# Linear attention and a squared-ReLU MLP on one core: moving two features, two sets of transposes and one batch of loads in a hand-written order

## The chip, the core and the metric

The kernel runs on one core of a Trainium2 chip. Its time is the device time of one execution in microseconds (us); given is the median of several runs. One execution was also profiled: its record gives the span, from the first to the last instruction, and its own time, which is a little longer.

The engines of the core run beside one another, each in its own order: TensorE (PE, with PEld for its weight loads), VectorE (DVE), ScalarE (ACT), GpSimd (POOL) and SyncE (SP). An engine waits on semaphores for what it needs, and everything behind a waiting instruction on that engine waits too. SP here only issues DMAs; POOL issues others.

## The reference

```python
r = np.maximum(x, 0.0)                                  # phi(x), x = q or k
phi = np.concatenate([r * cos, r * sin], axis=-1)       # cos, sin by position
kv  = np.einsum('bhsf,bhsd->bhfd', k_p, v)
z   = np.sum(k_p, axis=2)
num = np.einsum('bhsf,bhfd->bhsd', q_p, kv)
den = np.einsum('bhsf,bhf->bhs', q_p, z)[..., None] + 1e-06
x   = (num / den)            # then (batch*seq, heads*dim) = (4608, 512)
h   = x @ w_in               # 512 -> 2048
g   = relu(h) ** 2
out = g @ w_out              # 2048 -> 512, float32
```

q, k and v are float32 of (8 batches, 8 heads, 576 positions, 64 dims).

## The kernel before

The 576 positions of a batch are cut into four pieces of 128 positions (`j` = 0 to 3, all 8 heads) and a tail of 64 positions (`j` = 4, two groups of 4 heads on the two halves of the partitions). For each batch the work is:

- `load_batch`: one DMA of 1 MB and two of 64 KB for each of q, k and v. The input tiles have two buffers each.
- `att_k`: for a piece of k, a cosine half (relu, then times a column; on VectorE by `feat_cos`, L171, or on ScalarE by `feat_cos_act`, L186) and a sine half (`feat_sin`, ScalarE, L181). `att_v` copies v into bf16 beside a column of ones (L198 or L200).
- `att_kv`: 40 small matmuls into `kz` (L241), part 0 for j = 0 and 1, part 1 for the rest, then a copy to `kvz` on ScalarE (L249). The ones give the sum z.
- `att_feat` and `att_qT`: the same features for q, and a transposing DMA on SP (L267), one for j = 0 and 1, one for 2 and 3, one for the tail.
- `att_d`: `att_num`, 8 matmuls (L310), then `att_div` on VectorE (L320 to L324), which gives x. `att_x`: x is transposed by a DMA on SP (L342).
- `gemm1`: x times w_in in steps of 8 or 10 per batch. Each step's matmuls (L383) fill a PSUM tile `hps`, ScalarE takes its relu (`rt`, L391), VectorE squares it (`gT`, L398). `hps` has two buffers, so step n + 2 needs rt of step n.
- `gemm2`: g times w_out. From batch 1's second pair of row tiles on it is done by `pair_mm`, in which seven products of half-size blocks take the place of eight; it needs sums of blocks (`g_sum`, L521, and `w2_sum`, L506, on VectorE), copies of partial products on ScalarE (`s`, L561 and L576) and additions on VectorE (`u`, `ysb`, L537). Two of its four PSUM tiles (`yu`, `yv`) are in the two buffers of `hps`.

The order of the work is written out by hand. The main loop runs over **slots**: one slot is one step of gemm1 or gemm2. Slots 0 to 7 are gemm1 of batch 0, 8 to 15 its gemm2; 16 to 25 gemm1 of batch 1 and 26 to 33 its gemm2; 34 to 41 gemm1 of batch 2, 42 to 49 its gemm2; 50 to 59 gemm1 of batch 3. The attention of a later batch is hung behind these slots with `at(slot, function, ...)`. Within a slot the pieces run in the order of the `at` calls; the square of a gemm1 step follows its slot's pieces. `plan(b, k, f, kv, d, ...)` takes the slots of one batch: k for the key and value pieces, f for the query features and their transposes, kv for the two parts of kz, d for num, division and x transposes.

Each engine gets its instructions in this order. So SP, too, issues its DMAs strictly in order: query transposes, x transposes and, from batch 4 on, the loads. The loads of batches 1 to 3 go through POOL.

PSUM has one more buffer of note: `kz` and `num` share one (`pa`), so each needs the reader of the one before to be done.

Of the kernel before, what the change touches and what calls it, by code (L numbers as in the profile page):

```python
# [19 lines left out]
def kernel(  # L20
# [9 lines left out]
    nc = tc.nc  # L30
# [13 lines left out]
    NS = J + 1  # L44
# [562 lines left out]
    slots, first, second = [], {}, {}  # L607
# [6 lines left out]
    def at(s, fn, *args):  # L614
        after.setdefault(s, []).append((fn, args))
# [6 lines left out]
        att_qT_pe(b, j)  # L622
        att_qT_copy(b, j)

    def plan(b, k, f, kv, d, t=(), x=(), shared=True):


        for j in range(NS):
            last = j == J or j % 2
            at(k[j], att_k, b, j, feat_cos_act if shared and j % 2 else feat_cos)  # L630
            at(k[j], att_v, b, j, nc.scalar if shared and (b > 2 or j % 2) else nc.vector)
            at(f[j], att_feat, b, j)
            if t:
                at(t[j], att_t, b, j)
            elif last:
                at(f[j], att_qT, b, j // 2)
            at(d[j], att_d, b, j)
            if x:
                at(x[j], att_x_pe, b, j, x[j] > 16)
            elif last:  # L640
                at(d[j], att_x, b, j // 2)
        for i in range(2):
            at(kv[i], att_kv, b, i)


    for j in (2, 3):
# [8 lines left out]
    at(18, att_d, 0, J)  # L655
    at(19, att_x_pe, 0, J, True)
    plan(
        1,
        k=(8, 8, 8, 9, 9),
        f=(4, 5, 6, 12, 13),  # L660
        kv=(10, 10),
        d=(11, 13, 15, 17, 19),
        t=(5, 6, 7, 16, 17),
        x=(12, 14, 16, 18, 20),
        shared=False,
    )
    at(14, load_batch, 3, nc.gpsimd, "qkv")
    plan(
        2,
        k=(21, 22, 23, 24, 25),  # L670
        f=(18, 19, 20, 22, 23),
        kv=(26, 26),
        d=(27, 28, 29, 31, 33),
    )
    plan(
        3,
        k=(30, 32, 33, 34, 35),
        f=(27, 29, 31, 32, 33),
        kv=(36, 36),
        d=(37, 38, 39, 40, 41),  # L680
    )
    for b in range(4, B):
        o, p = second[b - 2], first[b - 1]
        at(second[b - 3] + 6, load_batch, b, nc.sync, "kv")
        at(first[b - 2] + 9, load_batch, b, nc.sync, "q")
        plan(
            b,
            k=(o, o, o + 1, o + 1, o + 2),
            f=(o + 4, o + 4, o + 5, o + 5, o + 6),
            kv=(o + 3, o + 4),  # L690
            d=[p + j for j in range(NS)],
        )
# [96 lines left out]
```

## Time and profile before

| what | value |
|---|---|
| median of 5 runs | 293.88 us (293.3 to 295.98) |
| the profiled execution's own time | 294.83 us |
| its span | 293.0 us |
| granted clock of TensorE | 1.0 throughout |
| TensorE busy | 281.2 us |
| VectorE busy | 201.6 us |
| ScalarE busy | 164.7 us |
| GpSimd busy | 39.2 us |

Busy shares are averages over the whole span. The waits of an engine say after whom it stood idle and for how long. In the timeline a row gives start, length, engine, line, operation and tile, and behind it in brackets the idle time just before and what ended it. An instruction's length there is longer than the distance to the next one on the same engine, since neighbours overlap: ScalarE's sine or cosine of a full piece takes 0.71 us and the next one starts after 0.61. DMA rows of SP show how long issuing took; the landing is told apart from it.

### The profile page before, as it was taken

How to read it: one execution, taken by the hardware profiler on the slowest of the kernel's cores; microseconds unless marked ns; L12 is line 12 of the kernel's file. 1: busy time of each engine (PE TensorE's matmuls, PEld its weight loads, DVE VectorE, ACT ScalarE, POOL GpSimd, SP SyncE). 2: the span in 40 equal slices, each digit the busy share in tenths (PEclk: the TensorE clock that was granted, in tenths of full speed). 3: DMA queues.
4: the chain of work that ended last, by engine and by line, in shares of the span. 5: the costliest groups of instructions: out<-in, count | busy, mean ns of one | idle time of the engine just before them, and what ended most of it. 6: DMA issues, size and time to landing. Idle time of an engine off the chain costs nothing.

```text
span 293.0 us, 7285 instructions
## 1 busy us (share of the span) xinstructions
PE 281.2 (96%) x3038; PEld 236.4 (81%) x3045; DVE 201.6 (69%) x450; ACT 164.7 (56%) x251; POOL 39.2 (13%) x67
## 2 busy tenths in 40 slices
PE   8989999998999979999999999999999999999994
PEld 3569855888677968898998888988998988889883
DVE  1367765596399486977688686977677877546584
ACT  3476653679748747745693258845595551155210
POOL 1462504750000000000002000000001000000011
PEclk9999999999999999999999999999999999999999
DMA  6999995999749988799619995199808520300014
GB/s 213 284 204 284 354 214 170 342 361 266 133 116 162 289 146 155 214 284 285 183 59 194 271 258 165 74 242 322 231 6 200 146 46 2 138 7 2 0 73 144
DMA packets 76641, 53.04 MB, mean 181 GB/s; under 512 B 52000, under 2 KB 71712, under 8 KB 76608
## 3 DMA queue, kind: packets, MB, share of 16 engines
q1 hardware_dynamic: 66816, 29.24, 43.4%
q0 software_dynamic: 9648, 23.20, 26.8%
q8 instruction: 24, 0.39, 0.5%
q10 hardware_dynamic: 144, 0.13, 0.1%
q14 instruction: 9, 0.07, 0.1%
HBM read 36.70 MB, written 9.44 MB: 157 GB/s over the span
## 4 chain that ended last, share of the span: by engine, by line
PE 83%; DVE 5%; DMA 5%; ACT 3%; SPq 2%; issue 1%; DVEq 0%
PE hps L383 41%; PE ya L525 9%; PE yc L525 8%; PE yu L525 7%; PE yv L525 4%; PE num L310 3%; DMA q<-in_q_dram 3%; PE kz L241 3%; PE yps L432 2%; PE yh L432 2%; PE yps L456 2%; DMA qpT<-qpt 2%; DVE ysb L537 1%; ACT rt L391 1%; PE tq L284 1%; SPq L69 1%
## 5 line engine op out<-in xcount | busy, mean ns | idle before, releaser
L383 PEld LDWEIGHTS <-w1sb 128*128 128x128 bf16 x1312 | 112.9, 98 | 13.7 <-issue 2.9
L383 PE MATMUL hps<-xT,w1sb 128*128 128x256 bf16 (+1 forms) x1056 | 119.0, 269 | 1.1 <-DVE ysb L537 0.6
L391 ACT ACTIVATE rt<-hps 128x1024 bf16<-128x1024 f32 x72 | 73.6, 1023 | 66.8 <-PE hps L383 43.4
L398 DVE TENSOR_TENSOR gT<-rt 128x1024 bf16<-128x1024 bf16 x64 | 44.0, 687 | 21.3 <-ACT rt L391 21.2
L525 PEld LDWEIGHTS <-gs 128*128 128x128 bf16 x480 | 46.9, 98 | 5.5
L525 PEld LDWEIGHTS <-gT 128*128 128x128 bf16 x312 | 29.8, 98 | 3.5
L410 POOL DMA_DIRECT2D out_dram<-ysb x14 | 7.6, 547 | 174.4 <-DVE ysb L537 146.9
L181 ACT ACTIVATE kp<-k,sin_col 128x512 bf16<-128x512 f32 x32 | 22.4, 717 | 3.1 <-DMA k<-in_k_dram 3.1
L324 DVE TENSOR_TENSOR x<-num,rden 128x512 bf16<-128x512 f32 x32 | 22.1, 691 | 1.1
L181 ACT ACTIVATE qp<-q,sin_col 128x512 bf16<-128x512 f32 x32 | 22.1, 721 | 1.2 <-DMA q<-in_q_dram 1.2
L320 DVE TENSOR_SCALAR den<-num 128x8 f32<-128x8 f32 (+1 forms) x40 | 6.6, 164 | 22.3 <-PE num L310 22.3
L521 DVE TENSOR_TENSOR gs<-gT 128x1024 bf16<-128x1024 bf16 x26 | 17.8, 685 | 0.0
L171 DVE TENSOR_SCALAR qp<-q,cos_col 128x512 bf16<-128x512 f32 x32 | 14.7, 487 | 1.7 <-DMA q<-in_q_dram 1.7
L383 PE MATMUL hps<-xTt,w1sb 128*128 128x128 bf16 x256 | 15.1, 219 | 0.8 <-ACT rt L391 0.8
L525 PE MATMUL yc<-w2sb,gs 128*128 128x256 bf16 x120 | 15.6, 272 | 0.0
L525 PE MATMUL yu<-w2sb,gs 128*128 128x256 bf16 x120 | 15.6, 272 | 0.0
L525 PE MATMUL ya<-w2t,gs 128*128 128x256 bf16 x120 | 15.6, 273 | 0.0
L525 PE MATMUL yu<-w2t,gs 128*128 128x256 bf16 x120 | 15.5, 272 | 0.0
L200 ACT CAST vext<-v 128x512 bf16<-128x512 f32 x23 | 14.1, 614 | 1.9 <-DMA v<-in_v_dram 1.9
L576 ACT COPY s<-yu 128x256 f32<-128x256 f32 x15 | 5.6, 372 | 16.7 <-PE yu L525 16.7
L310 PEld LDWEIGHTS <-qpT 128*128 128x128 bf16 (+1 forms) x240 | 10.3, 100 | 5.1 <-DMA qpT<-qpt 2.8
L310 PE MATMUL num<-kvz,qpT 128*128 128x65 bf16 (+1 forms) x240 | 11.7, 194 | 2.6 <-DMA qpT<-qpt 2.6
(93 smaller groups left out, 338.1 us busy)
## 6 DMA issues: line engine op xcount, KB each, us to landing
out_dram<-ysb POOLq DMA_DIRECT2D x14, 512.0 KB, 3.9
k<-in_k_dram SPq DMA_DIRECT2D x5, 1024.0 KB, 7.9
v<-in_v_dram SPq DMA_DIRECT2D x5, 1024.0 KB, 8.5
q<-in_q_dram SPq DMA_DIRECT2D x5, 1024.0 KB, 5.5
q<-in_q_dram POOLq DMA_DIRECT2D x3, 1024.0 KB, 12.4
k<-in_k_dram POOLq DMA_DIRECT2D x3, 1024.0 KB, 9.9
v<-in_v_dram POOLq DMA_DIRECT2D x3, 1024.0 KB, 10.0
w1sb<-in_moe_w_in_dram POOLq DMA_DIRECT2D x4, 512.0 KB, 9.3
```

The lines of the kernel that those rows point to most:

```text
L171: nc.vector.tensor_scalar(out=dst[:, :, 0:D], in0=src, scalar1=0.0, scalar2=cos_col[:, j : j + 1], op0=ALU.max, op1=ALU.mult,)
L181: nc.scalar.activation(out=dst[:, :, D:F], in_=src, func=ACTF.Relu, scale=sin_col[:, j : j + 1])
L200: copy(out=vx[:, j, h0:h1, 0:D], in_=piece("v", b, j)[:, h0:h1, :])
L241: nc.tensor.matmul(out=kz[:, half, hh * E1 : (hh + 1) * E1], lhsT=lhsT, rhs=rhs, start=(j == 0 and hh == 0), stop=(j == J and hh == HH - 1),)
L310: nc.tensor.matmul(out=out, lhsT=lhsT, rhs=kvz[:, half * HH + hh, :], start=True, stop=True)
L324: nc.vector.tensor_tensor(out=x_of(b, j).rearrange("p (b k) (l d) -> p b k l d", b=n, l=2), in0=n4[:, :, :, 0:D].rearrange("p b (k l) d -> ...
L383: nc.tensor.matmul(out=out, lhsT=w1sb[:, kb, hb * P : (hb + 1) * P], rhs=rhs, start=(kb == 0), stop=(kb == KB - 1),)
L391: nc.scalar.activation(out=rt[:, :, :], in_=hps[:, :, :], func=ACTF.Relu)
L398: nc.vector.tensor_tensor(out=dst, in0=rt[:, :, :], in1=rt[:, :, :], op=ALU.mult)
L432: nc.tensor.matmul(out=ypss[b][tt], lhsT=gTs[b][:, hb, tt * P : (tt + 1) * P], rhs=w2sb[:, hb, :], start=(hb == 0), stop=(hb == HB - 1),)
L521: nc.vector.tensor_tensor(out=t[:, :, :], in0=in0, in1=in1, op=op)
L525: nc.tensor.matmul(out=acc, lhsT=lhs[:, hb, :], rhs=rhs[:, hb, :], start=(hb == 0), stop=(hb == HB2 - 1),)
```

## The change

Four groups of slots and engines in the plan change; no instruction is added or taken away but for the engine that does some features.

- Batch 2: the cosine halves of k for j = 1 and 3 go from ScalarE to VectorE. All else of batch 2 stays.
- Batch 3: the cosine halves of k for j = 0, 1 and 2 are on ScalarE (before: 1 and 3), the rest on VectorE. The key pieces and the query features take other slots; query pieces 2, 3 and the tail are in slots 33 and 34 (before 31 to 33), and both of their transposes in slot 34. Part 1 of kz goes from slot 36 to 37. The nums and divisions go from slots 37 to 41 to slots 38 to 41 and 43, with their x transposes.
- Batch 4: the loads of k and v go from slot 32 to 34, where they stand behind batch 3's query transposes. On SP the order was: transpose of query pieces 2 and 3, k, kt, kt, v, vt, vt, transpose of batch 2's last x, transpose of the query tail. It becomes: transpose of batch 2's last x, of query pieces 2 and 3, of the query tail, then k, kt, kt, v, vt, vt.
- Batch 4's q stays in slot 43, but on SP it now comes after the tail x transpose of batch 3, which is in the same slot.

```diff
-    def plan(b, k, f, kv, d, t=(), x=(), shared=True):
+    def plan(b, k, f, kv, d, t=(), x=(), act_cos=(1, 3), act_v=range(NS)):
         for j in range(NS):
             last = j == J or j % 2
-            at(k[j], att_k, b, j, feat_cos_act if shared and j % 2 else feat_cos)
-            at(k[j], att_v, b, j, nc.scalar if shared and (b > 2 or j % 2) else nc.vector)
+            at(k[j], att_k, b, j, feat_cos_act if j in act_cos else feat_cos)
+            at(k[j], att_v, b, j, nc.scalar if j in act_v else nc.vector)
...
         x=(12, 14, 16, 18, 20),
-        shared=False,
+        act_cos=(),
+        act_v=(),
     )
...
         kv=(26, 26),
         d=(27, 28, 29, 31, 33),
+        act_cos=(),
+        act_v=(1, 3),
     )
     plan(
         3,
-        k=(30, 32, 33, 34, 35),
-        f=(27, 29, 31, 32, 33),
-        kv=(36, 36),
-        d=(37, 38, 39, 40, 41),
+        k=(29, 31, 32, 34, 35),
+        f=(27, 30, 33, 34, 34),
+        kv=(36, 37),
+        d=(38, 39, 40, 41, 43),
+        act_cos=(0, 1, 2),
     )
     for b in range(4, B):
         o, p = second[b - 2], first[b - 1]
-        at(second[b - 3] + 6, load_batch, b, nc.sync, "kv")
+        at(34 if b == 4 else second[b - 3] + 6, load_batch, b, nc.sync, "kv")
         at(first[b - 2] + 9, load_batch, b, nc.sync, "q")
```

## The prediction

> **What bounds the kernel now.** I read the shares of busy time first, then the chain that ended last, then the waits of TensorE, then the timeline of each engine in the stretch that the diff touches (64 to 126 us).
>
> ```profile
> PE 281.2 (96%) x3038; PEld 236.4 (81%) x3045; DVE 201.6 (69%) x450; ACT 164.7 (56%) x251; POOL 39.2 (13%) x67
> ...
> PE 83%; DVE 5%; DMA 5%; ACT 3%; SPq 2%; issue 1%; DVEq 0%
> ```
>
> TensorE (PE) is busy for 281.2 of 293.0 us at full granted clock. No edit here takes a matmul away, so only its idle time can be won. Its waits, in the waits of TensorE:
>
> ```profile
> PE num L310 <- DMA qpT<-qpt: 2.6, 1, 2.6
> ...
> PE hps L383 <- ACT rt L391: 0.8, 1, 0.8
> PE hps L383 <- DVE ysb L537: 0.6, 1, 0.6
> ...
> PE kz L241 <- ACT kpt L181: 0.3, 1, 0.3
> ```
>
> All four lie in the stretch of the edits. In the timeline, each stands in brackets after the instruction that it delayed; columns are start, length, engine, line:
>
> ```profile
> 72.74 1.95 PE L383 MATMUL hps<-xTt,w1sb 128*128 128x128 bf16 x32 [0.84 <-ACT rt L391]
> ...
> 77.71 0.30 PE L241 MATMUL kz<-vextt,kpt 64*128 64x65 bf16 x8 [0.32 <-ACT kpt L181]
> ...
> 91.26 5.40 PE L383 MATMUL hps<-xT,w1sb 128*128 128x256 bf16 x48 [0.63 <-DVE ysb L537]
> ...
> 110.31 0.32 PE L310 MATMUL num<-kvz,qpT 128*64 128x65 bf16 x8 [2.56 <-DMA qpT<-qpt]
> ```
>
> Together 4.35 us. SyncE's queue in the timeline says why the last one is so late:
>
> ```profile
> 92.34 1.59 SPq L267 DMA_TRANSPOSE qpT<-qp  x1
> 94.03 1.64 SPq L64 DMA_DIRECT2D k<-in_k_dram  x1
> 95.76 1.57 SPq L69 DMA_DIRECT2D kt<-in_k_dram  x2
> 97.44 0.87 SPq L64 DMA_DIRECT2D v<-in_v_dram  x1
> 98.41 4.82 SPq L69 DMA_DIRECT2D vt<-in_v_dram  x2
> 103.33 2.24 SPq L342 DMA_TRANSPOSE xTt<-xt  x1
> 105.67 3.40 SPq L267 DMA_TRANSPOSE qpT<-qpt  x1
> ```
>
> The tail features of batch 3's queries were ready at 93.9 (cosine 93.59 + 0.35), but their transpose stood behind six loads of batch 4 and went out at 105.67; it landed 4.6 us later.
>
> **Part 1: batch 2's cosines to VectorE (slots 22 and 24).** Two ScalarE passes of 0.71 us go; on its timeline one follows another every 0.61. Between 66.65 and 77.15 ScalarE never waits, so this shifts its work: rt of slot 23 starts at 71.68 - 0.61 = 71.07, and the matmul that waited for it gains 0.61. By the last kpt pass 1.22 is gone, the matmul row before it only moved by 0.61, so the 0.32 wait goes whole. Gain 0.61 + 0.32 = 0.93. VectorE takes two passes of 0.48, at 70 and 73 us: it idles 0.66, 1.58 and 1.23 us there, each time for rt, and the squares that follow wait for rt anyway. Without that cover they would cost 0.8. GpSimd is unaffected: it issues nothing from 64.9 to 84.7.
>
> **Part 2: batch 3's features (slots 27 to 35).** The 0.63 wait at 91.26 is VectorE running late: the row `u<-ya` at 89.81 stands behind the division and a query cosine. Ahead of it now lie three fewer passes of batch 3 (k at 87.04, q at 85.44 and 89.41) and one more (q, in slot 30): 2 x 0.40 less. In the old frame u starts at 89.0, the next u waits for yc (89.57), and ysb ends at 90.44; TensorE ends its previous matmul at 90.63. The wait goes: 0.63.
>
> Here a rule speaks against the change. The Trainium skill ("ScalarE: Activation LUTs", "Rules for kernel authors") says that relu and mul belong on VectorE, not ScalarE. The rows agree on the length (0.48 against 0.72 us), but the place decides: VectorE is what TensorE waits for at 91.26, while ScalarE idles 2.73, 1.12 and 0.78 us around there. By the rule the cosines stay and 0.63 is lost; by the rows it is won. I take the rows.
>
> ScalarE does pay in slot 34. After rt (slot 34; 1.95 after its matmuls begin, as 93.21 to 91.26) come k sine, v, and now two query sines: 0.92 + 0.61 + 0.51 + 0.62 + 0.40 = 3.06 before the next rt, where it was 2.65. Also only half of batch 3's kz (16 matmuls, 0.49) stands ahead of slot 37's matmuls, which need that rt's buffer. In new time slot 34 begins at 90.63 - 0.93 = 89.7; rt of slot 35 ends at 89.7 + 1.95 + 3.06 + 1.02 = 95.7; TensorE is there at 89.7 + 5.24 + 0.49 = 95.4. New wait: 0.3 (0 to 0.7). The other half of kz, now in slot 37, only moves.
>
> **Part 3: transposes ahead of the loads.** Both transposes of slot 34 follow their last sine, at 94.4 and 94.8; they issue near 94.5 and 96.5 (1.6 and 1.2 to 2 us each) and land by 99.5 and 101.5 (4.7 and 4.6). Their matmuls come in slots 40 and 43, about 104 and 110. So the 2.56 goes, with over 4 us to spare.
>
> What wins: 0.93 + 0.63 + 2.56 - 0.3 = 3.8. The moved num (0.25) is paid again in slot 43. Slot 42 then begins at 110.56 - 3.8 - 0.25 = 106.5 =: t.
>
> **What is late next.** Six loads of batch 4 (k, two kt, v, two vt) go out near 97.8 instead of 94.03, while their users come 4 us earlier. Behind them on SyncE: x transposes, then q's three loads, which now also stand behind the tail transpose of slot 43.
>
> v first. From k's issue to v's landing took 14.1 us in this batch (97.44 + 10.7 - 94.03), and 10.8, 14.0 and 11.2 in batches 5, 6, 7. So v lands at 108.6 to 111.9. ScalarE's first v copy is due at t + 2; behind it in the queue stand 2.26 us of work and the copy of yu, which TensorE must have at t + 5.5. The copy may begin as late as t + 2.85 = 109.35; each later microsecond is lost whole. Cost 0 to 2.5. The new order (two transposes, tail transpose, then k) is that of batches 5 and 7, so I lean to 11: none. Here too a rule differs: the Trainium skill ("DMA: Bandwidth & Descriptors", "Anatomy of one DMA") gives 2.0 us plus bytes at 436 GB/s; the 2.25 MB of k, v and tails would be an estimated 7.2 us, landing at 105.0 with no risk at all. The rows (10.8 to 14.1) decide.
>
> q second. Before, its landing at 119.49 made ScalarE wait 0.5 us at no cost. Now the last division of batch 3 follows the num of slot 43: num ends t + 3.75, xt is ready 0.9 later, the tail transpose takes 1.2 on SyncE (median; 2.24 at worst), then q goes out at t + 6.05 and lands 5.4 later (5.5, 5.4, 5.2 seen) at t + 11.45. After it come two sines, kvz, and the s copy (2.17 us together) before yu of slot 49, due at t + 12.92: 0.7 lost. VectorE says the same (two cosines and ysb, 1.3, against t + 12.05: 0.7). Batch 4's first query transpose then goes out 1.4 after q and lands 4.0 later, where TensorE would want it 5.15 after q: 0.3 more. So 1.0, up to 1.8 with the long transpose, and nothing if q lands 1 us sooner. The waits for v and q do not add; the later one counts. I take 1.2.
>
> Sum: 3.8 - 1.2 = 2.6. The profiled run took 294.83 (span 293.0 and 1.8 around it); the median shown is 293.88, 0.95 less. I take the gain from both: 292.2 for a run like the profiled one, **291.3** as the median. Past slot 50 the order is as before and PE-bound, so the gain stays.
>
> **The rivals.**
> Nothing is given back: q lands early enough (its tail transpose or load a microsecond faster), v within 11.5 us. Then 3.8: 290.1. For it: two of four batches had v within 11.2. Against: q's chain has no slack in the rows.
> The loads give most of it back: v takes 14 us again and costs 2.5, or SyncE is still held by the loads when the tail transpose comes (2.24 and 3.40 us at 103.33 and 105.67), and q costs 2 to 3. Then 1 us is left: 292.9. For it: two of four batches had v at 14 us.
> It ends slower: batch 4's v arrives so late that ScalarE's copy in slot 42 holds yu by more than was won. It eats the whole gain at v = 109.35 + 3.8 = 113.2 and makes 0.5% at 114.7, that is 16.9 us after k's issue; 17.5 us give 295.9. For it: DMA share is 1.0 in the stretches around the loads. Against: 14.1 is the longest of four.
> That the edit doesn't do what it says (the transpose still late) would need it to land after 110, 15 us after its sine: I count it in the third case.
>
> **How the numbers follow.** Chances 0.45 (291.3; its own range 290.4 to 292.2), 0.20 (290.1), 0.26 (292.9), 0.09 (295.9). Half a per cent, 1.47 us, is about what a measurement of this kernel tells from no change. Faster than 292.4: the first two and a fifth of the third, 0.70; slower than 295.35: 0.09; the rest 0.21. The range, 289.7 to 294.1, runs from nothing given back (and no wait in slot 37) to all given back in the third case.
>
> **What would show it.** The waits of TensorE lose all four rows above. New rows: hps waiting for rt near 95.4, and yu or yc near 118 waiting for the s copy or ysb behind q's landing. SyncE's queue shows qpt issued by 97 and k after it. I am wrong if num still waits for its transpose, if v lands past 113, or if a wait appears between slots 37 and 41.

## The result and the profile after

The changed kernel takes 292.51 us (median of 41 runs, 291.26 to 300.69), the kernel before 293.93 (median of 78). The ratio is 0.9944, 95% interval 0.9931 to 0.9958: faster by 0.56%, that is by 1.65 us (1.2 to 2.0). The prediction had 291.3, a gain of 2.6. The one run at 300.69 us, at a granted clock of 0.985 on average, is a slow one and is not in the ratio.

The profiled execution took 293.13 us, its span 291.3, at a granted clock of 0.997. These are the busy time and the chain of its page:

```profile
PE 281.5 (97%) x3038; PEld 236.0 (81%) x3045; DVE 201.9 (69%) x451; ACT 163.8 (56%) x250; POOL 39.0 (13%) x67
...
PE 79%; DMA 12%; DVE 3%; ACT 2%; POOL 2%; issue 1%; SPq 1%; DVEq 0%; ACTq 0%
```

TensorE is as busy as before; only its idle time can have changed. These are its waits in the stretch of the edits, in the timeline of the kernel after:

```profile
73.02 1.95 PE L383 MATMUL hps<-xTt,w1sb 128*128 128x128 bf16 x32 [0.23 <-ACT rt L391]
...
96.53 1.91 PE L383 MATMUL hps<-xT,w1sb 128*128 128x256 bf16 x16 [0.18 <-ACT rt L391]
...
120.42 1.03 PE L525 MATMUL yc<-w2sb,gs 128*128 128x256 bf16 x8 [0.89 <-DVE ysb L537]
...
122.53 1.91 PE L383 MATMUL hps<-xT,w1sb 128*128 128x256 bf16 x16 [0.20 <-DVE ysb L537]
```

Of the four waits of before, 0.23 of one is left; the three others are gone. Three new ones stand there: 0.18 before slot 37, and 0.89 and 0.20 where batch 4's q is late. SyncE's queue after, in the timeline:

```profile
92.22 1.43 SPq L342 DMA_TRANSPOSE xTt<-xt  x1
95.20 1.56 SPq L267 DMA_TRANSPOSE qpT<-qp  x1
96.85 1.26 SPq L267 DMA_TRANSPOSE qpT<-qpt  x1
98.16 0.58 SPq L64 DMA_DIRECT2D k<-in_k_dram  x1
98.85 1.75 SPq L69 DMA_DIRECT2D kt<-in_k_dram  x2
100.70 0.55 SPq L64 DMA_DIRECT2D v<-in_v_dram  x1
101.35 1.99 SPq L69 DMA_DIRECT2D vt<-in_v_dram  x2
104.69 5.75 SPq L342 DMA_TRANSPOSE xT<-x  x2
112.03 1.17 SPq L342 DMA_TRANSPOSE xTt<-xt  x1
113.25 0.58 SPq L64 DMA_DIRECT2D q<-in_q_dram  x1
```

The query tail goes out at 96.85 in place of 105.67 and is used at 110.81. And q goes out only behind the tail x transpose, which waits until 112.03 for the late division. Who waits for q, from the waits of ScalarE and of VectorE in this stretch:

```profile
ACT qp L181 <- DMA q<-in_q_dram: 3.5, 1, 3.5
```

```profile
DVE qp L171 <- DMA q<-in_q_dram: 1.7, 1, 1.7
```

**The two profiles and the two medians do not say the same.** The parts of the program ahead of the first edit differ from one execution to another: in the profile after, a matmul there (at 41.51) waits 0.57 us for the DMA that loads a part of w_out, which the profile before does not show. I therefore measure each profile from the matmuls of slot 21 on, which are the last ahead of the first edit, to the end of the span, and call this the stretch. In the timeline of before and of after they begin so:

```profile
64.71 5.40 PE L383 MATMUL hps<-xT,w1sb 128*128 128x256 bf16 x48
```

```profile
65.60 5.40 PE L383 MATMUL hps<-xT,w1sb 128*128 128x256 bf16 x48
```

Before, the stretch is 293.0 - 64.7 = 228.3 us; after, 291.3 - 65.6 = 225.7. That is 2.6 us, the same as the predicted gain, while the medians show 1.4 and the ratio 1.65. Where the other microsecond is was the first question for the experiments.

### The profile page after: what moved, and what is told of

Its sections match the earlier page's. It is cut to its first block, busy times and chain, and to the rows that moved or that the text cites. A ratio compares the mean times of both kernels' runs of the same rounds, so it can differ in the third digit from the quotient of the medians.

```text
span 291.3 us, 7285 instructions
## 1 busy us (share of the span) xinstructions
PE 281.5 (97%) x3038; PEld 236.0 (81%) x3045; DVE 201.9 (69%) x451; ACT 163.8 (56%) x250; POOL 39.0 (13%) x67
## 4 chain that ended last, share of the span: by engine, by line
PE 79%; DMA 12%; DVE 3%; ACT 2%; POOL 2%; issue 1%; SPq 1%; DVEq 0%; ACTq 0%
PE hps L383 37%; PE ya L525 9%; PE yc L525 9%; PE yu L525 7%; DMA q<-in_q_dram 5%; PE yv L525 4%; DMA w2sb<-in_moe_w_out_dram 4%; PE num L310 3%; DMA v<-in_v_dram 3%; PE kz L241 3%; PE yps L456 2%; PE yh L432 2%; PE yps L432 2%; DVE ysb L537 1%; POOL w1sb L117 1%
## 5 line engine op out<-in xcount | busy, mean ns | idle before, releaser
L391 ACT ACTIVATE rt<-hps 128x1024 bf16<-128x1024 f32 x72 | 73.6, 1023 | 65.6 <-PE hps L383 44.1
L200 ACT CAST vext<-v 128x512 bf16<-128x512 f32 x23 | 14.1, 615 | 2.0 <-DMA v<-in_v_dram 2.0
L525 PE MATMUL yc<-w2sb,gT 128*128 128x256 bf16 x104 | 13.5, 273 | 0.0
L525 PE MATMUL yv<-w2t,gT 128*128 128x256 bf16 x104 | 13.5, 273 | 0.0
```

Of the source, the lines that this page charges most:

```text
L200: copy(out=vx[:, j, h0:h1, 0:D], in_=piece("v", b, j)[:, h0:h1, :])
L391: nc.scalar.activation(out=rt[:, :, :], in_=hps[:, :, :], func=ACTF.Relu)
L525: nc.tensor.matmul(out=acc, lhsT=lhs[:, hb, :], rhs=rhs[:, hb, :], start=(hb == 0), stop=(hb == HB2 - 1),)
```

## The experiments

**Both kernels once more.**

> The kernel before, unchanged, to see how much its waits differ from one execution to another. The profiled pair shows a gain of 2.6 us in the part of the program from the first edit on (span 293.0 less 64.7, against 291.3 less 65.6), the medians only 1.4. Theory A: the wait of num for its transpose depends on how the DMAs of that execution fall, and 2.56 was on the long side: this profile shows 1.0 to 2.2 in its place, and the four waits come to 3.0 to 3.9 in place of 4.35. Theory B: the four waits are the same within 0.2 us in every execution, and the difference lies in the early part of the program or in the changed kernel. Ratio 1.00 either way.

Measured: 293.51 against 293.36 us for the kernel before beside it, ratio 1.002 (0.9988 to 1.0052). The stretch is 226.9 us, 1.4 shorter than in the first profile of the same kernel. The waits in this second timeline of the kernel before:

```profile
72.88 1.95 PE L383 MATMUL hps<-xTt,w1sb 128*128 128x128 bf16 x32 [0.84 <-ACT rt L391]
77.85 0.30 PE L241 MATMUL kz<-vextt,kpt 64*128 64x65 bf16 x8 [0.33 <-ACT kpt L181]
91.39 5.40 PE L383 MATMUL hps<-xT,w1sb 128*128 128x256 bf16 x48 [0.62 <-DVE ysb L537]
109.08 0.32 PE L310 MATMUL num<-kvz,qpT 128*64 128x65 bf16 x8 [1.21 <-DMA qpT<-qpt]
```

Three waits repeat within 0.01 us: what makes them is the order of instructions on the engines. The fourth is 1.21 where it was 2.56. SyncE's queue shows where the difference arises:

```profile
103.31 1.22 SPq L342 DMA_TRANSPOSE xTt<-xt  x1
104.64 1.20 SPq L267 DMA_TRANSPOSE qpT<-qpt  x1
```

Here the two transposes behind the loads were issued in 1.22 and 1.20 us; in the first profile it took 2.24 and 3.40. Take the wait for the transpose off, and the stretches of the two profiles are 228.3 - 2.6 = 225.7 and 226.9 - 1.2 = 225.7. So between these two profiles the kernel before differs by this one wait, and the profile that I predicted from had a long one.

> The changed kernel, unchanged. Theory A (its gain is steady, the wait of the kernel before varies): yc waits 0.7 to 1.1 us for ysb behind q's landing as in the first profile (0.89), no other wait over 0.3 from the first edit on. Theory B (the changed kernel varies): yc or yu waits 1.5 us or more in this execution, or v lands after ScalarE wants it. Ratio 0.994 to 0.995.

Measured: 292.56 against 293.36 us, ratio 0.9978 (0.9952 to 1.0003). That misses the 0.994 to 0.995 that I expected: here the gain is 0.8 us by the medians, and no gain at all is not excluded. The interval only just meets that of the first measurement (0.9931 to 0.9958), so the size of the gain is less certain than the first interval alone says. The stretch is 225.6 against 225.7 in the first profile; yc waits 0.75 and hps 0.20. So the changed kernel's waits repeat, as Theory A has it; its ratio did not.

**The loads behind the transposes, alone.** On the kernel before:

```diff
-        at(second[b - 3] + 6, load_batch, b, nc.sync, "kv")
+        at(34 if b == 4 else second[b - 3] + 6, load_batch, b, nc.sync, "kv")
```

> The kernel before with one edit: batch 4's k and v loads in slot 34 in place of 32, so behind both query transposes; features, engines and divisions stay. If the 2.56 us wait comes from the loads standing ahead of the tail's transpose: it goes whole, nothing takes its place (q's transpose partner is early here, v may land until 110.8), and the time falls by 1.7 to 2.5 us: ratio 0.9915 to 0.994. If the transposes are slow for another reason: the wait stays over 1.5 and the ratio is within 0.002 of 1.

Measured: 291.87 us, ratio 0.9952 (0.9926 to 0.9978). The wait for the transpose is gone, the three others stay (0.84, 0.33, 0.62), no new one comes. The stretch is 225.7: just that of before without its wait. The time fell by 1.5 us, a little less than the expected 1.7 to 2.5; three profiles of the kernel with this wait have 2.56, 1.21 and 1.77 there, so an average run probably loses less than 2.56.

This run says more than that one step is right. It has a single edit, and its stretch is the 225.7 of the whole change; its median on the same chip (291.87) is no worse than the whole change's (292.56). The other edits' gains (batch 2's and batch 3's cosines) and their costs (q, and the wait before slot 37) about cancel, as 0.93 + 0.63 - 0.3 - 1.2 = 0.06 in the prediction's own sum.

**Batch 2's cosines on VectorE, alone.** On the kernel before:

```diff
-            at(k[j], att_k, b, j, feat_cos_act if shared and j % 2 else feat_cos)
+            at(k[j], att_k, b, j, feat_cos_act if shared and b > 2 and j % 2 else feat_cos)
```

> The kernel before with part 1 alone: batch 2's two cosines on VectorE. If the step of the prediction holds: hps waits 0.2 for rt in place of 0.84, kz no longer waits for kpt (0.3), both waits further on (0.6 for ysb and 1.2 to 2.6 for the transpose) stay, since TensorE comes to the transpose 0.9 earlier and its DMAs do not all come earlier: the later wait may take up to 0.9 back. Time 0.2 to 0.9 us below the kernel before: ratio 0.997 to 0.9995. If the gain passes through whole: the wait for the transpose is no longer than 1.2 to 2.6 and the ratio is 0.997; if it is swallowed there: the ratio is 1.000.

Measured: 292.44 against 293.69 us, ratio 0.9948 (0.9917 to 0.9978), so the gain was not swallowed. The fall of 1.25 us is more than the 0.2 to 0.9 I expected, but the interval, up to 0.9978, reaches into that range. The waits that are left, in its timeline:

```profile
71.94 1.95 PE L383 MATMUL hps<-xTt,w1sb 128*128 128x128 bf16 x32 [0.23 <-ACT rt L391]
90.06 5.40 PE L383 MATMUL hps<-xT,w1sb 128*128 128x256 bf16 x48 [0.61 <-DVE ysb L537]
108.30 0.32 PE L310 MATMUL num<-kvz,qpT 128*64 128x65 bf16 x8 [1.77 <-DMA qpT<-qpt]
```

The stretch is 226.4, or 224.6 without the 1.77 of this execution: 1.1 below the 225.7 of before, to about 0.1, since spans are given in tenths. The waits that went sum to 0.61 + 0.33 + 0.01 = 0.95. The prediction had 0.93 for this part. And here is a third value for the transpose's wait: 2.56, 1.21, 1.77.

**Batch 3's cosines on VectorE again.** On the changed kernel:

```diff
-        act_cos=(0, 1, 2),
+        act_cos=(),
```

> The changed kernel with batch 3's three cosines back on VectorE, where the rule for relu and mul puts them; slots as changed. By the timeline: two more passes (0.8) ahead of u in VectorE's queue, so ysb ends 0.6 late and hps waits 0.5 to 0.7 for it at the head of slot 34 again; the wait of 0.2 for rt before slot 37 stays or goes; q's chain takes part of it back, since TensorE then comes to yc later. Ratio to the kernel before 0.995 to 0.997 (the changed kernel 0.9944). If VectorE is not what counts there: no wait at the head of slot 34 and the time of the changed kernel.

Measured: 292.91 us, ratio 0.9957 (0.9934 to 0.998), which alone does not tell it from the changed kernel. The timeline does:

```profile
89.36 5.40 PE L383 MATMUL hps<-xT,w1sb 128*128 128x256 bf16 x48 [0.61 <-DVE ysb L537]
95.43 1.91 PE L383 MATMUL hps<-xT,w1sb 128*128 128x256 bf16 x16 [0.18 <-ACT rt L391]
119.61 1.03 PE L525 MATMUL yc<-w2sb,gs 128*128 128x256 bf16 x8 [1.19 <-DVE ysb L537]
```

The wait at the head of slot 34 is back at 0.61, as expected. I had thought that q's chain would return part of it; that was a miss. The likely reason, which no run isolates, is that the chain begins at a num on TensorE and so is as late as TensorE is; yc waited longer still (1.19), q having taken 6.2 us to land where it had taken 5.9 and 5.7. The stretch is 226.7, 1.0 more than the changed kernel's.

**q earlier.** On the changed kernel:

```diff
-        at(first[b - 2] + 9, load_batch, b, nc.sync, "q")
+        at(40 if b == 4 else first[b - 2] + 9, load_batch, b, nc.sync, "q")
```

> The changed kernel with one edit: batch 4's q is loaded in slot 40 in place of 43, so that on SyncE it stands behind one x transpose only and no longer behind the transpose of the late tail division. If q's place behind that transpose is what gives a part of the gain back: the waits of yc (0.89) and hps (0.20) go, q lands by 115, and the time falls by 0.9 to 1.3 us below the changed kernel: ratio to the kernel before 0.989 to 0.991. If the next thing after q is just as late (v on ScalarE, the x transposes now behind q): no faster than the changed kernel, ratio 0.994.

> The kernel with q loaded in slot 40, again, beside the next one on the same chip. Ratio to the kernel before 0.989 to 0.992; from the first edit on 224.3 to 224.8 us.

Measured: 290.62 us against 293.36, ratio 0.9897 (0.9871 to 0.9923), and again, 290.97 against 293.95, 0.9882 (0.9844 to 0.992). The stretch is 224.5 both times, 1.1 below the changed kernel. SyncE's queue of the first of the two:

```profile
103.62 1.37 SPq L342 DMA_TRANSPOSE xT<-x  x1
105.05 0.57 SPq L64 DMA_DIRECT2D q<-in_q_dram  x1
105.73 1.42 SPq L69 DMA_DIRECT2D qt<-in_q_dram  x2
108.13 1.57 SPq L342 DMA_TRANSPOSE xT<-x  x1
```

q leaves at 105.05 and lands 6.1 us later; the waits of yc and hps (0.20) are gone, while those of 0.23 and 0.18 before them stay. So what the changed kernel gives back at q is 1.1 us, and it is not replaced by another wait.

**Is it the late division that holds q?** On the changed kernel, first with the tail in slot 41, then in slot 42:

```diff
-        d=(38, 39, 40, 41, 43),
+        d=(38, 39, 40, 41, 41),
```

> The changed kernel with one edit: batch 3's tail num, division and transpose in slot 41 in place of 43; q stays in slot 43. If the late tail division is what makes q late on SyncE: q goes out 2 to 3.5 us earlier, the waits of yc (0.75 to 0.89) and hps (0.2) go, no wait comes before the tail's num, and the time is that of the run with q loaded early, 0.9 to 1.3 below the changed kernel: ratio 0.989 to 0.991. If q is late because of the loads of k and v ahead of it: q goes out within 1 us of where it did, and the ratio stays at 0.994.

Measured: 294.18 us, ratio 1.0003 (0.997 to 1.0036), slower than the changed kernel. This edit was badly made, and the timeline says how:

```profile
83.46 0.62 PE L310 MATMUL num<-kvz,qpT 128*128 128x65 bf16 x8 [4.86 <-DMA qpT<-qp]
83.90 3.03 PE L456 MATMUL yps<-w2sb,gT 128*128 128x512 bf16 x8
...
112.18 0.42 PE L310 MATMUL num<-kvz,qpT 128*128 128x65 bf16 x8
114.50 0.32 PE L310 MATMUL num<-kvz,qpT 128*64 128x65 bf16 x8 [1.91 <-DVE x L324]
```

Two nums now follow one another in one slot, and they share one PSUM buffer; the second waits for the first one's division. That is 1.91 us lost for 1.1 at q. By this account it should be 0.8 us slower than the changed kernel, and the ratio is worse than that.

The profile has one more wait, 4.86 us for a query transpose of batch 2, at 83.46 and well ahead of the moved work; no other profile shows it, and what made this transpose late is open. It costs more than its own length. The granted clock is 1.00 from 80 to 82 us, 0.70 from 82 to 84, 0.50 from 84 to 86, 0.95 from 86 to 88 and 1.00 from then on, and the eight matmuls at 83.90 take 3.03 us where the same eight take 1.89 in the changed kernel (at 79.81). With the 0.62 of the num before them, for 0.41, that is another 1.35 us. The stretch of this profile is 297.2 - 64.5 = 232.7 us; less 4.86, 1.35 and 1.91 it is 224.6, which is what the kernel with q early takes (224.5). So the edit does free q, and the shared buffer takes more than that back.

The ratio may have the same cause. The profiled execution (299.04 us, mean clock 0.994) is the longest of the twelve. Of the other eleven, five had a mean clock of 0.997 or more and took 292.4 to 293.1 us, and six had 0.991 to 0.994 and took 293.8 to 295.9. Of the 29 executions of the kernel before beside them, four had 0.991 to 0.994, at 295.0 to 296.1. These have no trace, so that they too had a long wait is not shown; nor is it known whether the edit makes such executions more frequent.

```diff
-        d=(38, 39, 40, 41, 43),
+        d=(38, 39, 40, 41, 42),
```

> The changed kernel with one edit: batch 3's tail num, division and transpose in slot 42, one slot earlier; q stays in slot 43. The run with both in slot 41 had put two nums into one slot, and the second waited 1.9 us for the first one's division, since both use one PSUM buffer; here that wait can't be. If the tail division's place makes q late: q goes out 1.5 to 2 us earlier against TensorE's work, the waits of yc and hps go but for 0.2, and the part from the first edit on takes 224.4 to 224.9 us (changed kernel 225.6 and 225.7, q early 224.5); ratio to the kernel before 0.989 to 0.992. If the loads ahead of it do: a wait of 0.7 to 0.9 for q's features stays.

Measured: 291.74 us against 293.95, ratio 0.9909 (0.9874 to 0.9944). The wait of yc is gone; hps still waits 0.20, and the tail's num 0.17 for the division before it. The stretch is 225.1, 0.6 below the changed kernel, where I had expected 0.8 to 1.2. SyncE's queue and TensorE's remaining waits there:

```profile
110.05 1.44 SPq L342 DMA_TRANSPOSE xTt<-xt  x1
111.54 0.57 SPq L64 DMA_DIRECT2D q<-in_q_dram  x1
```

```profile
108.23 0.32 PE L310 MATMUL num<-kvz,qpT 128*64 128x65 bf16 x8 [0.17 <-DVE x L324]
120.84 1.91 PE L383 MATMUL hps<-xT,w1sb 128*128 128x256 bf16 x16 [0.20 <-DVE ysb L537]
```

From the start of the stretch (64.54) q goes out after 47.0 us, where the changed kernel has 113.25 - 65.60 = 47.65. That is 0.65 earlier and not the expected 1.5 to 2, and it fits the 0.6 won. So the late division holds q; giving it one slot less wins half of what moving q itself wins. I had also written that the wait for the shared PSUM buffer can't be here: 0.17 of it is left.

**A better version.** On the kernel with q in slot 40: batch 2's v copy for j = 1 on VectorE, and the tail query features, their transpose and the loads of k and v one slot later.

```diff
         act_cos=(),
-        act_v=(1, 3),
+        act_v=(3,),
...
-        f=(27, 30, 33, 34, 34),
+        f=(27, 30, 33, 34, 35),
...
-        at(34 if b == 4 else second[b - 3] + 6, load_batch, b, nc.sync, "kv")
+        at(35 if b == 4 else second[b - 3] + 6, load_batch, b, nc.sync, "kv")
```

> The kernel with q loaded early and two more small moves: batch 2's copy of v for j = 1 on VectorE, to take away the 0.23 that hps waits for rt; batch 3's tail query features, their transpose and with it the loads of batch 4 in slot 35, to take away the 0.18 before slot 37. If both waits go and nothing follows: 0.3 to 0.5 us below the run with q early, ratio 0.988 to 0.989. If the loads, 1 to 2 us later, now hold ScalarE's copy of v in slot 42: equal to it or 0.5 to 1.5 slower, with a wait of ScalarE for v.

> The kernel with q early and the two further moves, again. If the two small waits (0.23 and 0.18) and what hung on them are really saved: 0.4 to 0.9 us less than the run with q early from the first edit on, and a ratio of 0.987 to 0.990. If the one profile of it was lucky: the two kernels are equal within 0.3 us.

Measured: 290.78 us against 293.69, ratio 0.9883 (0.9838 to 0.9928), and 290.21 against 293.95, 0.9856 (0.9821 to 0.9892). In both profiles TensorE has no wait over 0.1 us in the window from 64 to 130 us, and the stretch is 223.7 and 223.6, 0.9 below the kernel with q early. Beside that kernel on the same chip its median is 0.76 lower. The two waits that were to go make 0.41 of these 0.9, and I had expected 0.3 to 0.5; where the other half was is not shown, as the kernel with q early has no other wait of 0.1 us or more there. The ratios' intervals overlap, so the stretches carry this verdict. Against the changed kernel the stretches of the two versions are clear: 1.1 and 2.0 us, each in two profiles of either kernel.

## Why the prediction was right, and where its size was off

Its sum was +0.93 + 0.63 + 2.56 - 0.3 - 1.2 = 2.6. Term by term:

| term | predicted | what the runs showed |
|---|---|---|
| ScalarE's backlog, slots 24 to 26 | 0.93 | 0.95 by its waits, 1.1 by the stretch (part 1 alone) |
| VectorE late at slot 34 | 0.63 | 0.63; it comes back at 0.61 with the cosines on VectorE |
| tail transpose behind the loads | 2.56 | gone whole; worth 2.56, 1.21 and 1.77 in three executions |
| new wait for rt before slot 37 | -0.3 | -0.18 |
| v late on ScalarE | 0 (to -2.5) | 0 |
| q late behind the division | -1.2 | -1.1 (rows 0.89 + 0.20; 1.1 by moving q) |

Every mechanism was there, and each at its place. The term that was mis-sized is the third: in "so the 2.56 goes", 2.56 was one execution's value of a wait that depends on how DMAs fall. The other two profiles have 1.2 and 1.8 in its place, and with these the sum is 1.3 to 1.8: the medians have 1.4, the ratio 1.65 (1.2 to 2.0). I had the sign of this before me: the profiled run took 294.83, 0.95 over the median, and "I take the gain from both" carried the whole gain over to the median, though an average run had not that much to win there. The three other waits repeat to 0.01 us, which I could not know from one profile, but could have guessed: they end on an engine's instruction that waits for no DMA, the fourth on a DMA's landing. (One sum has a gap: 3.75 + 0.9 + 1.2 is 5.85, so 0.2 of q's "t + 6.05" is given no source. And the gain of 2.6 that the two profiles show is no proof of the sum, since the first of them had the long wait that the sum was made from.)

The outcome at 292.5 lies outside the first case's own range (290.4 to 292.2) and beside my third case (292.9), but not by the third case's mechanism: the loads gave nothing back. v came at 107.4, sooner than the 108.6 to 111.9 that I had from the other batches. ScalarE did not wait for it.

On the two rules that I weighed: batch 3's cosines are better on ScalarE here, though each is slower there, as the run with them on VectorE shows in its 0.61. For v's landing I trusted the rows (10.8 to 14.1 us from k's issue); the new order gave 9.2 and 11.1 in the two profiles of the changed kernel, still more than the estimate of 7.2 from the formula of the Trainium skill ("DMA: Bandwidth & Descriptors", "Anatomy of one DMA"). The page fits that formula to single DMAs that GpSimd issues, and these are six that SyncE issues, so the difference does not speak against the page; I had stretched it.

## What to carry to other kernels

Before taking a wait from a profile into a sum, ask what ends it: here the waits for engine instructions that hung on no DMA repeated within 0.01 us, the wait for a DMA was 2.56, 1.21 and 1.77, and yc's wait for an instruction that itself hung on q's DMA was 0.89 and 0.75. The profiled run with the 2.56 was 0.95 us slower than the median: a sign that it had drawn a long wait. When work is moved later, follow every DMA that stands behind it in the same queue: here a division moved by two slots held q, whose place could be changed for nothing. Try each part of a change alone: one edit of the four had the whole net gain. And two users of a single PSUM buffer should not stand in one slot.

## What the runs showed of the hardware that I had not expected

The same loads land sooner when they stand behind the transposes. From the issue of k to the landing of v it took 14.1, 12.8 and 13.4 us in the three profiles with k going out right behind the query transpose of pieces 2 and 3, and 8.8 to 11.2 us in the other ten (9.2 and 11.1 in the changed kernel, 8.8 with the loads alone moved), where both query transposes were issued first and k goes out, in the changed kernel, 3.0 us after the larger one. That the overlap with this transpose's data makes the difference is likely, but no run here isolates it.

A long wait of TensorE was followed by a lower granted clock. In the run with both nums in slot 41, TensorE stood idle for 4.86 us, and its clock then fell to 0.50 and was back at 1.00 within 6 us; eight matmuls took 3.03 us in place of 1.89. After the wait of 2.56 us in the kernel before, the clock stayed at 1.00. One trace shows the fall, so where the limit lies is not known.
